# A four-layer transformer on one core: the first chunk and key weights turned on TensorE, key-phase weights kept resident, two chunks interleaved in the query phase, background matmuls on column tiles

## Chip, core, metric

The kernel runs on one core of one Trainium2 chip. The metric is device time in microseconds (us), the median of the runs; lower is better. The kernel before takes 2942.88 us (2942.56 to 2943.19, two runs).

PE is TensorE, ACT ScalarE, DVE VectorE. A "PSUM bank" is, in this kernel, one of the eight buffers of 512 columns that matmuls write to.

## The reference, cut to what matters

Four layers, A B A B, over x of 2048 rows by 1024 columns in bf16, 32 heads of 32. Both kinds have residuals and a layer norm.

```python
def _A_ref(x, wqkv, w_phi, wo):            # linear attention
    q, k, v = split(x @ wqkv)
    pq = einsum("bhsd,hdf->bhsf", q, w_phi); pk = the same of k
    phi_q = concat([softmax(pq), softmax(-pq)]); phi_k = the same of pk
    kv = einsum("bhsf,bhsd->bhfd", phi_k, v);  z = phi_k summed over s
    o = (phi_q @ kv) / (phi_q . z + 1e-6)
    return o @ wo

def _B_ref(x, wqkv, wo):                   # ordinary attention
    p = softmax(q @ k.T * Dh**-0.5)
    return (p @ v) @ wo

x = x + A(layernorm(x)); x = x + B(layernorm(x)); x = x + A(...); x = x + B(...)
```

I call an A with the B behind it one layer pair; there are two. The rows are handled in four chunks of 512.

## The kernel before

Each pair has a *key phase* (A's keys and values of all chunks), a *query phase* (A's queries, then B's projections), and *attention* (B). The first key phase runs alone at the start; the second pair's is done in the background of the first pair's attention. Attention consists of 512 steps per pair. One step is eight score matmuls S, two exponentials of 128x1024 on ACT, and sixteen matmuls ND that give numerators and denominators. Between S and ND of each step, PE takes some *background* work from a list of generators:

```python
LAYOUT = {"wide": (0, 8), "mid": (2, 3), "narrow": (3, 1)}   # score buffers of two banks, background banks

def ps512(dt=F32):                        # the next background bank
    PS["ring"] += 1
    return ps_tile(f"BG{PS['ring'] % PS['nb']}", ...)[:]

def mm8(ps, lhsT, rhs):                   # a block: 8 matmuls of 128x128 by 512 columns
    for po in range(G):
        PE.matmul(ps, lhsT=lhsT(po), rhs=rhs(po), start=(po == 0), stop=(po == G - 1))
        if po == 3:
            yield 4, False                # half done; (units of work, has a tile ended?)

def pump(self, per):                      # once per step
    self.credit = min(self.credit + per, 8.0)
    ends = 0
    while self.credit > 0 and ends < max(1, PS["nb"] - 1):
        got = self.next()
        if got is None:
            return
        self.credit -= got[0]
        ends += got[1]
...
for _ in block:                           # attend(): a step has just issued its S
    bg.pump(per)
    if len(att.lag) > 1:
        att.finish()                      # the ND of an earlier step
```

A unit of work is about one matmul of 512 columns; a tile *ends* when its bank is full and another engine can empty it. The attention layout "narrow" has three score buffers (six banks), one bank for ND and one for background. S uses tiles of 32 rows of the array (`tile_position=(32*j, 0)`), ND tiles of 32 columns (`(0, 32*j)`), background the whole array. Where a later stage needs background that isn't done, `bg.until(name)` runs the rest with no scores beside it. I call that stretch *bare*.

The start loads the first chunk and the key weights transposed, by DMA, alternating between two issuing queues, and the key phase loads its weight slabs (1 MB each) again for every chunk:

```python
def load_first(c):
    x = T("x", [P, G, C], BF16)
    for po in range(G):
        (SC if c == 0 and po % 2 else SP).dma_start_transpose(out=x[:, po, :], in_=A_x[0, ...])
    return x
...
xs = {0: load_first(0)}; load_phi(); wkT = fold_load(D, SC)    # fold_load: 8 more transposes, on SC
for c in range(NCH):
    sl = Slabs(["av", "pk"][:1 if c == 0 else 2])             # loads value and key slabs
```

The query phase of a chunk ends its sums with a chain of eleven small DVE instructions, among them one reciprocal of 3.35 us; nothing else is ready for PE in the meantime:

```python
DVE.tensor_copy(out=sdc[:], in_=sd)                        # aq_gen
...
DVE.reciprocal(out=t1[q0, :], in_=t1[q0, :])
...
DVE.tensor_tensor(out=ab[q3, :], in0=t2[q2, :], in1=ab[q2, :], op=ALU.subtract)
yield 8, True
yield from wait(6)
```

The softmax here doesn't subtract the row's maximum and nothing guards it: scores larger than these inputs give would overflow.

## Time and profile before

The head of the page gives the span and each engine's busy time, share of the span and number of instructions. No engine is busy throughout.

```profile
span 2935.6 us, 69119 instructions
...
PE 2365.3 (81%) x29739; PEld 1044.6 (36%) x30080; DVE 1336.3 (46%) x2205; ACT 2141.0 (73%) x2465; POOL 96.1 (3%) x87
```

A share over the whole span says little here, because the stages have different limits. I cut the trace at the score exponentials, which stand in a fixed order, and asked for each engine's busy time in each stage. First pair of the kernel before; columns: stretch, its length, busy us and instruction count of each engine, granted clock, DMA share, GB/s.

```profile
0.00:71.80 71.80, 8.25 (x17) 1.94 (x18) 9.55 (x67) 5.55 (x9) 0.86 (x9) 1.00 0.46 103
71.80:238.70 166.90, 150.28 (x931) 80.03 (x946) 115.20 (x185) 86.81 (x144) 47.52 (x38) 0.95 0.71 216
238.70:322.80 84.10, 69.40 (x290) 28.67 (x295) 50.01 (x80) 19.86 (x35) 0.00 (x0) 0.87 0.38 128
322.80:417.70 94.90, 77.82 (x928) 32.89 (x941) 44.24 (x77) 69.97 (x80) 0.00 (x0) 0.89 0.34 104
417.70:493.10 75.40, 67.34 (x301) 28.84 (x307) 38.52 (x61) 1.34 (x3) 0.00 (x0) 0.93 0.55 178
493.10:703.10 210.00, 173.73 (x2569) 74.61 (x2607) 81.42 (x148) 187.23 (x210) 0.00 (x0) 0.95 0.35 111
703.10:856.30 153.20, 122.25 (x1722) 52.41 (x1749) 73.36 (x139) 129.07 (x146) 0.00 (x0) 0.90 0.37 116
856.30:889.00 32.70, 23.34 (x126) 9.69 (x120) 8.97 (x13) 0.04 (x1) 0.00 (x0) 1.00 0.51 153
```

The reader should see four kinds of stretch. The start (first line) has nothing busy. The key and query phases (second and third) are PE's. The fifth and eighth lines are bare: ACT does next to nothing. In between, ACT and PE share. ACT alone would need about 1.85 us per step; 160 steps (lines six to eight) took 396 us, not 296.

What holds the start is told by the chain that ended last, in order of time (start, us, what):

```profile
11.40 2.56 DMA x<-in_A_x_dram
...
13.97 2.58 DMA x<-in_A_x_dram
...
27.03 3.27 DMA kv<-in_A_wqkv_dram
...
31.49 2.79 DMA x<-in_A_x_dram
```

One transpose lands, and only then does the next, from the other queue, begin: 2.6 us each. The Trainium skill, "DMA: Bandwidth & Descriptors", section "Silent corruption: two transposing streams in flight at once", says that the later of two transposing streams must wait for the earlier one's full completion. The trace agrees: the transpose of 11.40 us ends at 13.96, and the next begins at 13.97.

Last, one step of the first block (layout "mid"), PE alone (start, us, line, out<-in, count):

```profile
354.59 0.40 PE L534 MATMUL S<-q,kv 32*128 32x256 bf16 x8
354.92 1.90 PE L163 MATMUL BG<-c,w 128*128 128x512 bf16 x8
356.75 0.29 PE L561 MATMUL ND<-E,kv 128*32 128x256 bf16 x4
...
357.31 0.40 PE L534 MATMUL S<-q,kv 32*128 32x256 bf16 x8
```

The step takes 2.71 us. Between the start of the last background matmul and the first ND, the trace has 0.309 us (the median of the 673 such places after 400 us), though a matmul of 512 columns takes 0.216.

### The profile page before, as it was taken

How to read it: one execution, taken by the hardware profiler on the slowest of the kernel's cores; microseconds unless marked ns; L12 is line 12 of the kernel's file. 1: busy time of each engine (PE TensorE's matmuls, PEld its weight loads, DVE VectorE, ACT ScalarE, POOL GpSimd, SP SyncE). 2: the span in 40 equal slices, each digit the busy share in tenths (PEclk: the TensorE clock that was granted, in tenths of full speed). 3: DMA queues.
4: the chain of work that ended last, by engine and by line, in shares of the span. 5: the costliest groups of instructions: out<-in, count | busy, mean ns of one | idle time of the engine just before them, and what ended most of it. 6: DMA issues, size and time to landing. Idle time of an engine off the chain costs nothing.

```text
span 2935.6 us, 69119 instructions
## 1 busy us (share of the span) xinstructions
PE 2365.3 (81%) x29739; PEld 1044.6 (36%) x30080; DVE 1336.3 (46%) x2205; ACT 2141.0 (73%) x2465; POOL 96.1 (3%) x87
## 2 busy tenths in 40 slices
PE   1897978789777888888878797878978778988877
PEld 0453333333333333333333333333333333333333
DVE  1676454433546744454522745444254573322212
ACT  0552542889858888898996346188986699999996
POOL 0230000000000001010100100000000000000000
PEclk9998989999898998998999898999989899999999
DMA  4862616234253432323212261633424432321110
GB/s 101 241 213 85 194 62 197 76 129 138 67 165 111 122 127 87 120 79 114 73 45 101 79 194 59 197 93 123 134 75 147 125 97 100 105 73 59 45 45 16
DMA packets 259090, 323.98 MB, mean 110 GB/s; under 512 B 49568, under 2 KB 223648, under 8 KB 251616
## 3 DMA queue, kind: packets, MB, share of 16 engines
q1 hardware_dynamic: 248160, 316.93, 33.8%
q8 instruction: 235, 3.85, 0.5%
q10 hardware_dynamic: 10624, 2.62, 0.5%
q14 instruction: 71, 0.58, 0.1%
HBM read 252.77 MB, written 58.33 MB: 106 GB/s over the span
## 4 chain that ended last, share of the span: by engine, by line
PE 51%; ACT 18%; DVE 16%; DMA 6%; issue 5%; SPq 3%; ACTq 1%; DVEq 0%; POOLq 0%; POOL 0%
PE BG L163 28%; ACT E L543 16%; PE ND L561 10%; PE S L534 9%; DVE rc L599 3%; DMA dn<-den_d 2%; SPq L501 2%; DVE c L180 2%; DMA x<-in_A_x_dram 1%; PE BG L197 1%; DVE st L191 1%; PE BG L310 1%; ACT ea L376 1%; DVE f L397 1%; DMA den_d<-dt 1%
## 5 line engine op out<-in xcount | busy, mean ns | idle before, releaser
L543 ACT ACTIVATE E<-S 128x1024 bf16<-128x1024 f32 x2048 | 1909.3, 1116 | 408.2 <-PE S L534 407.3
L561 PE MATMUL ND<-E,kv 128*32 128x256 bf16 x8192 | 652.8, 288 | 249.5 <-DVE dt L581 77.1
L163 PE MATMUL BG<-c,w 128*128 128x512 bf16 x2371 | 591.3, 385 | 59.2 <-issue 20.2
L534 PE MATMUL S<-q,kv 32*128 32x256 bf16 x8192 | 564.2, 284 | 78.6 <-ACT E L543 40.7
L561 PE MATMUL ND<-E,ones 128*32 128x256 bf16 x8192 | 586.5, 286 | 0.0
L561 PEld LDWEIGHTS <-kv 128*32 128x32 bf16 x8192 | 266.5, 97 | 655.6 <-issue 523.5
L163 PE MATMUL BG<-w,c 128*128 128x512 bf16 x1442 | 355.6, 387 | 34.9 <-DVE st L463 12.4
L163 PEld LDWEIGHTS <-w 128*128 128x128 bf16 x2560 | 228.4, 99 | 342.9 <-issue 126.6
L534 PEld LDWEIGHTS <-kv 32*128 32x128 bf16 x8192 | 169.8, 92 | 408.5 <-issue 406.0
L561 PEld LDWEIGHTS <-ones 128*32 128x32 bf16 x8192 | 262.3, 99 | 5.1
L599 DVE RECIPROCAL rc<-nd 128x256 f32<-128x256 f32 x128 | 224.4, 1753 | 4.4
L163 PEld LDWEIGHTS <-c 128*128 128x128 bf16 x1536 | 142.4, 99 | 212.1 <-issue 60.7
L440 DVE TENSOR_TENSOR x<-BG,x 128x512 bf16<-128x512 f32 x128 | 88.4, 691 | 191.2 <-PE BG L163 190.8
L592 DVE COPY nd<-ND 128x512 f32<-128x512 f32 x64 | 44.1, 689 | 261.8 <-PE ND L561 261.3
L294 POOL TENSOR_TENSOR ea<-ea,sm 128x512 bf16<-128x512 bf16 x64 | 93.8, 1465 | 791.8 <-ACT E L543 339.6
L189 ACT ACTIVATE st<-c 128x512 bf16<-128x512 bf16 x56 | 31.5, 622 | 118.2 <-DMA xa_d<-c 65.0
L412 DVE TENSOR_TENSOR ea<-BG,ea 128x512 bf16<-128x512 f32 x128 | 84.7, 686 | 56.5 <-PE BG L411 38.7
L376 ACT ACTIVATE ea<-f 128x512 bf16<-128x512 f32 x128 | 75.3, 660 | 39.9 <-DVE f L373 39.8
L197 PE MATMUL BG<-st,ones 128*128 128x512 bf16 x121 | 48.5, 489 | 67.1 <-ACT st L189 51.0
L288 DVE TENSOR_REDUCE sm<-ea 128x32 f32<-128x1024 bf16 x64 | 77.8, 1216 | 53.1 <-ACT ea L284 35.3
L373 DVE TENSOR_TENSOR f<-BG,r 128x512 f32<-128x512 f32 x64 | 44.0, 691 | 125.8 <-PE BG L163 125.8
L463 DVE TENSOR_SCALAR st<-BG,rcol 128x512 bf16<-128x512 f32 x64 | 48.0, 751 | 97.5 <-PE BG L163 97.5
(79 smaller groups left out, 1238.4 us busy)
## 6 DMA issues: line engine op xcount, KB each, us to landing
w<-in_B_wqkv_dram SPq DMA_DIRECT2D x48, 1024.0 KB
dn<-den_d SPq DMA_DIRECT2D x320, 64.0 KB
w<-in_A_wqkv_dram SPq DMA_DIRECT2D x16, 1024.0 KB
x_d<-x SPq DMA_DIRECT2D x16, 1024.0 KB
x<-x_d SPq DMA_DIRECT2D x16, 1024.0 KB
w<-wpq_d SPq DMA_DIRECT2D x16, 1024.0 KB
w<-in_A_wo_dram SPq DMA_DIRECT2D x16, 1024.0 KB
w<-in_B_wo_dram SPq DMA_DIRECT2D x16, 1024.0 KB
```

Source lines behind the costliest of these rows:

```text
L163: PE.matmul(ps, lhsT=lhsT(po), rhs=rhs(po), start=(po == 0), stop=(po == G - 1))
L180: DVE.tensor_tensor(out=xc[:, po, :], in0=x[:, po, :], in1=m[:], op=ALU.subtract)
L197: PE.matmul(ps, lhsT=ones_bf[:], rhs=sqs[po], start=(po == 0), stop=(po == G - 1))
L288: DVE.reduce_sum(out=ss[:], in_=e[:].rearrange("p s (h f) -> p s h f", f=DH), axis=AX.X)
L294: (POOL if s else DVE).tensor_tensor(out=e[:, s, :].rearrange("p (h f) -> p h f", f=DH), in0=e[:, s, :].rearrange("p (h f) -> p h f", f=DH ...
L376: SC.activation(out=e[:, s, :], in_=pq[:], func=ACT.Exp, scale=1.0 - 2.0 * s)
L412: DVE.tensor_tensor(out=es[g][:, s, :], in0=ps, in1=es[g][:, s, :], op=ALU.mult)
L440: DVE.tensor_tensor(out=x[:, ft, :], in0=ps, in1=x[:, ft, :], op=ALU.add)
L534: PE.matmul(tiles[j // 2][:, o:o + QH], lhsT=kv[rows, 0, (kc + k) * P:(kc + k + 1) * P], rhs=q[rows, g, half * QH:(half + 1) * QH], start= ...
L543: SC.activation(out=e[:], in_=tiles[i][:].rearrange("p (j k q) -> p j k q", k=2, q=QH), func=ACT.Exp, scale=SCALE,)
L561: PE.matmul(nd[rows, part * QH:(part + 1) * QH], lhsT=ones_bf[:, 0:32] if part else kv[:, 1, col:col + 32], rhs=es[j // 2][:, j % 2, i, :] ...
L599: DVE.reciprocal(out=rc[:], in_=ndc[:, QH:C])
```

## The change

Its intent, in five parts: (1) the first chunk is loaded in rows and turned on TensorE, the key weights too; (2) the key phase's slabs stay in memory; (3) the query phase is cut into parts, so that chunk 1's exponents fill chunk 0's waits, and less is left to the background of the first block; (4) background beside attention runs as four tiles of 32 columns, the shape of ND; (5) the background is paced differently: three tile ends per step in "mid", and in the first 96 of the 160 narrow steps 5 units per step instead of 4, with chunks 2 and 3 queued together. A few smaller edits come with it (some query-phase results are emptied by ACT and no longer by DVE, the query weights are loaded one chunk earlier).

```diff
+    def mm(ps, lhsT, rhs, start, stop):
+        if PS["ns"] == 0:
+            PE.matmul(ps, lhsT=lhsT, rhs=rhs, start=start, stop=stop, skip_group_check=True)
+            return
+        for j in range(4):
+            cols = slice(32 * j, 32 * j + 32)
+            PE.matmul(ps[cols, :], lhsT=lhsT[:, cols], rhs=rhs, start=start, stop=stop,
+                      tile_position=(0, 32 * j), skip_group_check=True)
 ...
-            while self.credit > 0 and ends < max(1, PS["nb"] - 1):
+            while self.credit > 0 and ends < PS["nb"]:
 ...
-        xs = {0: load_first(0)}
-        wkT = fold_load(D, SC)
+        wn = [T("q", [P, 4, D], BF16) for _ in range(2)]    # key weights, as they lie
+        av = [T("kv", [P, G, C], BF16) for _ in range(2)]   # resident value and
+        pk = [T("w", [P, G, C], BF16) for _ in range(2)]    # folded key slabs
+        ...  # plain loads; load_first(0) and fold_k turn them with PE.transpose
-            main = ak_gen(c, xs[c], sl, True, res, hook)
+            main = ak_gen(c, xs[c], iter(av + pk).__next__, True, res, hook)
 ...
-            drain(to_b(0, (0,), True))
 ...
+            drain(aq_exp(xr0, wpq, es0))
+            exp1 = aq_exp(xr1, wpq, es1)
+            drain(aq_scale(es0, r0))
+            for _ in range(8):
+                next(exp1)
 ...
+            drain(merge(aq_out(es0, r0), exp1, 6))
+            drain(aq_scale(es1, r1))
+            drain(aq_finish(0, x0, r0["sl"], r0))
 ...
             bg.add("b2", to_b(2))
+            bg.add("b3", to_b(3))
-            attend(att, att.block(qs[0], 4, 8, acc[0], None, False, False), bg, 4)
-            attend(att, att.block(qs[1], 0, 8, acc[1], None, True, False), bg, 4)
+            attend(att, att.block(qs[0], 4, 8, acc[0], None, False, False), bg, 5)
+            attend(att, att.block(qs[1], 0, 8, acc[1], None, True, False), bg, 5)
             bg.until("b2")
-            bg.add("b3", to_b(3))
```

More of the change, by code (lines that the diff above doesn't have):

```diff
@@ L153, in ps512 @@
         PS["ring"] += 1
-        return ps_tile(f"BG{PS['ring'] % PS['nb']}", C if dt == F32 else P, dt)[:]
+        return ps_tile(f"BG{PS['ring'] % PS['nb']}", C, dt)[:]
     def wait(n):
@@ L159, in wait @@
             yield 0, True
+    def mm(ps, lhsT, rhs, start, stop):
[4 more added lines that the diff above has]
+            cols = slice(32 * j, 32 * j + 32)
+            PE.matmul(
+                ps[cols, :], lhsT=lhsT[:, cols], rhs=rhs, start=start, stop=stop,
+                tile_position=(0, 32 * j), skip_group_check=True,
+            )
     def mm8(ps, lhsT, rhs):
         for po in range(G):
-            PE.matmul(ps, lhsT=lhsT(po), rhs=rhs(po), start=(po == 0), stop=(po == G - 1))
+            mm(ps, lhsT(po), rhs(po), po == 0, po == G - 1)
             if po == 3:
@@ L196, in ln_gen @@
         for po in range(G):
-            PE.matmul(ps, lhsT=ones_bf[:], rhs=sqs[po], start=(po == 0), stop=(po == G - 1))
+            mm(ps, ones_bf[:], sqs[po], po == 0, po == G - 1)
             if po < G - 1 and po % 2:
@@ L234, in flush_kv, with ak_gen @@
             yield from pending.pop(0)()
-    def ak_gen(c, x, slabs, fast=False, res=None, hook=None):
+    def ak_gen(c, x, get, fast=False, res=None, hook=None):
         if c == 0:
@@ L239, in ak_gen @@
         kvacc = kv_state["acc"]
-        slabs.prefetch()
         if res is None:
@@ L252, in ak_gen @@
         for fc in range(2):
-            w = slabs.get()
+            w = get()
             for t in range(4):
@@ L267, in ak_gen @@
         for fc in range(2):
-            w = slabs.get()
+            w = get()
             es = []
@@ L309, in kv_part @@
                         for s in range(2):
-                            PE.matmul(
+                            mm(
                                 ps[:, s * 129:(s + 1) * 129],
-                                lhsT=es[t][:, s, gi * P:(gi + 1) * P],
-                                rhs=va[t // 2][:, t % 2, g, :],
-                                start=(t == 0 and s == 0), stop=(t == 3),
-                                skip_group_check=True,
+                                es[t][:, s, gi * P:(gi + 1) * P],
+                                va[t // 2][:, t % 2, g, :],
+                                t == 0 and s == 0, t == 3,
                             )
@@ L354, in kv_finish, with aq_load @@
         yield 0, True
-    def aq_gen(c, x, slabs, res, fast=False):
-        kvs, zs = kv_state["m"], kv_state["z"]
+    def aq_load(c):
         xc = T("c8", [P, G, C], BF16)
@@ L362, in aq_gen, with aq_exp @@
         SP.dma_start(out=rstd[:], in_=ra_d[c][:])
-        slabs.prefetch()
-        es = []
+        return xc, rstd
+    def aq_exp(xr, ws, es):
+        xc, rstd = xr
         for g in range(G):
-            if g % 4 == 0:
-                w = slabs.get()
+            if callable(ws):
+                w = ws() if g % 4 == 0 else w
+            else:
+                w = ws[g // 4]
             ps = ps512()
@@ L373, in aq_gen, with aq_scale @@
             DVE.tensor_tensor(out=pq[:], in0=ps, in1=rstd[:], op=ALU.mult)
-            e = T("ea", [P, 2, C], BF16)
             for s in range(2):
-                SC.activation(out=e[:, s, :], in_=pq[:], func=ACT.Exp, scale=1.0 - 2.0 * s)
-            es.append(e)
+                SC.activation(out=es[g][:, s, :], in_=pq[:], func=ACT.Exp, scale=1.0 - 2.0 * s)
             yield 4, True
+    def aq_scale(es, res):
+        zs = kv_state["z"]
         sd = ps512()
@@ L381, in aq_gen @@
             for s in range(2):
-                PE.matmul(
-                    sd[64 * s:64 * (s + 1), :], lhsT=zs[:, s, g, :], rhs=es[g][:, s, :],
-                    start=(g == 0), stop=(g == G - 1), tile_position=(0, 64 * s),
-                    skip_group_check=True,
-                )
+                for k in range(2):
+                    o = 64 * s + 32 * k
+                    PE.matmul(
+                        sd[o:o + 32, :], lhsT=zs[:, s, g, 32 * k:32 * k + 32],
+                        rhs=es[g][:, s, :], start=(g == 0), stop=(g == G - 1),
+                        tile_position=(0, o), skip_group_check=True,
+                    )
+            if g == 3:
+                yield 4, False
         sdc = T("f", [P, C], F32)
@@ L391, in aq_gen @@
         ab = T("ab", [P, C], BF16)
+        res["ab"] = ab
         q0, q1, q2, q3 = (slice(32 * i, 32 * i + 32) for i in range(4))
-        DVE.tensor_copy(out=sdc[:], in_=sd)
+        (SC.copy if PS["ns"] == 0 else DVE.tensor_copy)(out=sdc[:], in_=sd)
         DVE.tensor_tensor(out=t1[q0, :], in0=sd[q1, :], in1=sdc[q2, :], op=ALU.mult)
@@ L403, in aq_gen, with aq_out @@
         DVE.tensor_tensor(out=ab[q3, :], in0=t2[q2, :], in1=ab[q2, :], op=ALU.subtract)
-        yield 8, True
-        yield from wait(6)
-        oT = T("c8", [P, G, C], BF16)
+        yield 4, True
+    def aq_out(es, res):
+        kvs, ab = kv_state["m"], res["ab"]
+        oT = res["oT"] = T("c8", [P, G, C], BF16)
+        act = PS["ns"] == 0
         def bcast(g):
@@ L410, in bcast @@
                 ps = ps512()
-                PE.matmul(ps, lhsT=Rsel[:, g, s, :], rhs=ab[:], start=True, stop=True)
+                mm(ps, Rsel[:, g, s, :], ab[:], True, True)
                 DVE.tensor_tensor(
@@ L422, in aq_gen, with aq_finish @@
             for s in range(2):
-                PE.matmul(
-                    ps, lhsT=kvs[s][:, g, :], rhs=es[g][:, s, :], start=(s == 0), stop=(s == 1)
-                )
-            (SC.copy if fast else DVE.tensor_copy)(out=oT[:, g, :], in_=ps)
+                mm(ps, kvs[s][:, g, :], es[g][:, s, :], s == 0, s == 1)
+            (SC.copy if act else DVE.tensor_copy)(out=oT[:, g, :], in_=ps)
             yield 2, True
-        yield from proj_out(x, oT, slabs)
-        yield from ln_gen(x, res, fast)
+    def aq_gen(c, x, slabs, res, pause=6):
+        xr = aq_load(c)
+        slabs.prefetch()
+        es = [T("ea", [P, 2, C], BF16) for _ in range(G)]
+        yield from aq_exp(xr, slabs.get, es)
+        yield from aq_scale(es, res)
+        yield from wait(pause)
+        yield from aq_out(es, res)
+        yield from aq_finish(c, x, slabs, res)
+    def aq_finish(c, x, slabs, res):
+        yield from proj_out(x, res["oT"], slabs)
+        yield from ln_gen(x, res, PS["ns"] == 0)
         SP.dma_start(out=x_d[c][:], in_=x[:])
@@ L462, in bkv_gen @@
             )
-            DVE.tensor_scalar(
-                out=st[:, :, t, :], in0=ps.rearrange("p (g d) -> p g d", d=P),
-                scalar1=rcol[:, t:t + 1], scalar2=None, op0=ALU.mult,
+            scale_rows(
+                st[:, :, t, :], ps.rearrange("p (g d) -> p g d", d=P), rcol[:, t:t + 1],
+                PS["ns"] == 0,
             )
@@ L571, in finish @@
             if not last:
-                a = acc[0][g][:, acc[1], half, :]
+                a = acc[0][g // 2][:, g % 2, half, :]
                 if half == 0:
@@ L594, in finish @@
                 DVE.tensor_tensor(
-                    out=ndc[:, 0:QH], in0=num, in1=acc[0][g][:, acc[1], half, :], op=ALU.add
+                    out=ndc[:, 0:QH], in0=num, in1=acc[0][g // 2][:, g % 2, half, :], op=ALU.add
                 )
@@ L679, in run, with loads @@
         set_mode("wide")
-        xs = {0: load_first(0)}
+        wn = [T("q", [P, 4, D], BF16) for _ in range(2)]
+        av = [T("kv", [P, G, C], BF16) for _ in range(2)]
+        pk = [T("w", [P, G, C], BF16) for _ in range(2)]
+        xs = {}
+        res = {}
+        def loads():
+            SP.dma_start(out=av[0][:], in_=W["av"](0))
+            for k in range(2):
+                (SC if k else SP).dma_start(
+                    out=wn[k][:], in_=A_w[:, 4 * k:4 * k + 4, D:2 * D]
+                )
+            SP.dma_start(out=av[1][:], in_=W["av"](1))
+        xs[0] = load_first(0)
         load_phi()
-        wkT = fold_load(D, SC)
-        res = {}
+        loads()
         drain(ln_gen(xs[0], res, True))
@@ L686, in run @@
             nres = {}
-            sl = Slabs(["av", "pk"][:1 if c == 0 else 2])
             hook = None
             if c == 0:
-                hook = lambda sl=sl: fold_phi(wkT, wpk_d, sl)
-            if c == 2:
-                wqT = fold_load(0, SP)
+                hook = lambda: fold_k(wn, pk)
+            if c == 1:
+                wqT = [T("q", [P, 4, D], BF16) for _ in range(2)]
+                for g in range(G):
+                    SP.dma_start_transpose(
+                        out=wqT[g // 4][:, g % 4, :], in_=A_wqkv[:, g * P:(g + 1) * P]
+                    )
             if c == 3:
-                hook = lambda: fold_phi(wqT, wpq_d, None)
-            main = ak_gen(c, xs[c], sl, True, res, hook)
+                hook = lambda: fold_q(wqT)
+            main = ak_gen(c, xs[c], iter(av + pk).__next__, True, res, hook)
             if c + 1 < NCH:
@@ L709, in after @@
             if layer == 0:
-                yield from ak_gen(c, x, sl, fast)
+                yield from ak_gen(c, x, sl.get, fast)
                 SP.dma_start(out=x_d[c][:], in_=x[:])
@@ L723, in run @@
             drain(kv_finish())
-            tiles = [T(f"acc{g}", [P, 2, 2, QH], F32) for g in range(G)]
-            acc = [(tiles, 0), (tiles, 1)]
             qs = {}
@@ L730, in run, with to_b, b_proj @@
             BKVQ = ["bk0", "bv0", "bq0", "bk1", "bv1", "bq1"]
-            def to_b(c, parts=(0, 1), fast=False):
-                if 0 in parts:
-                    x = load_x(c)
-                    res = saved[c] = {}
-                    sl = res["sl"] = Slabs(["pq", "ao"] + (BKVQ if c < 2 else BKV))
-                    yield from aq_gen(c, x, sl, res, fast)
-                    if c < 2:
-                        qs[c] = T("q", [P, G, C], BF16)
+            def to_b(c):
+                x = load_x(c)
+                res = saved[c] = {}
+                sl = res["sl"] = Slabs(["pq", "ao"] + BKV)
+                yield from aq_gen(c, x, sl, res)
+                yield from b_proj(c, (0, 1))
+                SP.dma_start(out=xb_d[c][:], in_=res["xc"][:])
+                SP.dma_start(out=rb_d[c][:], in_=res["rstd"][:])
+            def b_proj(c, parts):
                 res = saved[c]
@@ L742, in to_b, with rest1 @@
                     yield from bkv_gen(c, res, res["sl"], h, qs.get(c))
-                if c >= 2:
-                    SP.dma_start(out=xb_d[c][:], in_=res["xc"][:])
-                    SP.dma_start(out=rb_d[c][:], in_=res["rstd"][:])
-            drain(to_b(0, (0,), True))
+            x0 = load_x(0)
+            r0, r1 = {}, {}
+            saved[0], saved[1] = r0, r1
+            r0["sl"] = Slabs(["ao"] + BKVQ)
+            r1["sl"] = Slabs(["ao"] + BKVQ)
+            sp = Slabs(["pq"])
+            xr0 = aq_load(0)
+            sp.prefetch()
+            wpq = sp.ready
+            es0 = [T("ea", [P, 2, C], BF16) for _ in range(G)]
+            early = [T(f"acc{4 + k}", [P, 2, 2, C], BF16) for k in range(4)]
+            es1 = [early[g // 2][:, g % 2] for g in range(G)]
+            xr1 = aq_load(1)
+            drain(aq_exp(xr0, wpq, es0))
[3 more added lines that the diff above has]
+                next(exp1)
+            r0["sl"].prefetch(1)
+            drain(merge(aq_out(es0, r0), exp1, 6))
+            drain(aq_scale(es1, r1))
+            drain(aq_finish(0, x0, r0["sl"], r0))
+            qs[0] = T("q", [P, G, C], BF16)
+            qs[1] = T("q", [P, G, C], BF16)
+            drain(b_proj(0, (0,)))
+            def rest1():
+                yield from aq_out(es1, r1)
+                x1 = load_x(1)
+                yield from aq_finish(1, x1, r1["sl"], r1)
+                yield from b_proj(1, (0, 1))
             bg = Background()
             set_mode("mid")
-            bg.add("b0", to_b(0, (1,)))
-            bg.add("b1", to_b(1))
+            bg.add("b0", b_proj(0, (1,)))
+            bg.add("b1", rest1())
+            acc = [([T(f"acc{k}", [P, 2, 2, QH], F32) for k in range(4)], 0), None]
             attend(
@@ L758, in run @@
             bg.until("b1")
+            acc[1] = ([T(f"acc{4 + k}", [P, 2, 2, QH], F32) for k in range(4)], 1)
             set_mode("narrow")
             bg.add("b2", to_b(2))
-            attend(att, att.block(qs[0], 4, 8, acc[0], None, False, False), bg, 4)
-            attend(att, att.block(qs[1], 0, 8, acc[1], None, True, False), bg, 4)
+            bg.add("b3", to_b(3))
+            attend(att, att.block(qs[0], 4, 8, acc[0], None, False, False), bg, 5)
+            attend(att, att.block(qs[1], 0, 8, acc[1], None, True, False), bg, 5)
             bg.until("b2")
-            bg.add("b3", to_b(3))
             attend(att, att.block(qs[0], 8, 12, acc[0], None, False, False), bg, 6)
@@ L812, with pe_transpose @@
     phi = T("t16", [P, G, P], BF16)
-    def fold_load(base, eng):
-        wT = [T("kv", [P, 4, D], BF16) for _ in range(2)]
-        for g in range(G):
-            eng.dma_start_transpose(
-                out=wT[g // 4][:, g % 4, :], in_=A_wqkv[:, base + g * P:base + (g + 1) * P]
-            )
-        return wT
-    def fold_phi(wT, dst, slabs):
-        ws = [T("w", [P, G, C], BF16) for _ in range(2)]
-        for hh in range(2):
-            for m in range(G):
-                ps = ps512()
-                for gi in range(4):
-                    PE.matmul(
-                        ps[:, gi * P:(gi + 1) * P],
-                        lhsT=wT[hh][:, gi, m * P:(m + 1) * P], rhs=phi[:, hh * 4 + gi, :],
-                        start=True, stop=True, skip_group_check=True,
-                    )
-                (DVE.tensor_copy if m % 2 else SC.copy)(out=ws[hh][:, m, :], in_=ps)
-                yield 1, True
-            SP.dma_start(out=dst[:, :, hh * C:(hh + 1) * C], in_=ws[hh][:])
-        if slabs is not None:
-            slabs.ready += ws
+    def pe_transpose(dst, src, k):
+        ps = ps512(BF16)
+        for i in range(4):
+            PE.transpose(out=ps[:, i * P:(i + 1) * P], in_=src(i), identity=ident[:])
+        (SC.copy if k % 2 else DVE.tensor_copy)(out=dst, in_=ps)
@@ new lines, in fold_k @@
+    def fold_k(wn, ws):
+        for hh in range(2):
+            wT = T("c8", [P, 4, D], BF16)
+            for gi in range(4):
+                o = (hh * 4 + gi) * P
+                for k in range(2):
+                    pe_transpose(
+                        wT[:, gi, k * C:(k + 1) * C],
+                        lambda i: wn[k][:, i, o:o + P], gi * 2 + k,
+                    )
+                    yield 1, True
+            yield from fold_mm(wT, hh, lambda m: ws[hh][:, m, :])
+            SP.dma_start(out=wpk_d[:, :, hh * C:(hh + 1) * C], in_=ws[hh][:])
@@ new lines, in fold_mm, with fold_q @@
+    def fold_mm(wT, hh, dst):
+        for m in range(G):
+            ps = ps512()
+            for gi in range(4):
+                PE.matmul(
+                    ps[:, gi * P:(gi + 1) * P],
+                    lhsT=wT[:, gi, m * P:(m + 1) * P], rhs=phi[:, hh * 4 + gi, :],
+                    start=True, stop=True, skip_group_check=True,
+                )
+            (DVE.tensor_copy if m % 2 else SC.copy)(out=dst(m), in_=ps)
+            yield 1, True
+    def fold_q(wT):
+        for hh in range(2):
+            st = T("st", [P, 4, C], BF16)
+            st2 = T("st", [P, 4, C], BF16)
+            yield from fold_mm(wT[hh], hh, lambda m: (st, st2)[m // 4][:, m % 4, :])
+            for i, t in enumerate((st, st2)):
+                SP.dma_start(out=wpq_d[:, 4 * i:4 * i + 4, hh * C:(hh + 1) * C], in_=t[:])
@@ L849, in load_first @@
         x = T("x", [P, G, C], BF16)
+        if c:
+            for po in range(G):
+                SP.dma_start_transpose(
+                    out=x[:, po, :], in_=A_x[0, c * C:(c + 1) * C, po * P:(po + 1) * P]
+                )
+            return x
+        rows = [T("ea", [P, D], BF16) for _ in range(4)]
+        for t in range(4):
+            (SC if t % 2 else SP).dma_start(out=rows[t][:], in_=A_x[0, t * P:(t + 1) * P, :])
         for po in range(G):
-            (SC if c == 0 and po % 2 else SP).dma_start_transpose(
-                out=x[:, po, :], in_=A_x[0, c * C:(c + 1) * C, po * P:(po + 1) * P]
-            )
+            pe_transpose(x[:, po, :], lambda i: rows[i][:, po * P:(po + 1) * P], po)
         return x
@@ L864, in store_out @@
             for po in range(G):
-                ps = ps512(BF16)
+                ps = ps512(BF16)[:, 0:P]
                 PE.transpose(out=ps, in_=x[:, po, t * P:(t + 1) * P], identity=ident[:])
```

## The prediction

Its "layer" is a layer pair, and its "value products" are ND.

> **What bounds it now.** The page shows ACT busy 73%, PE 81%. I cut the trace at the score exponentials (2048 of 128x1024, one every 0.93 us back to back: 1.86 us per attention step of two).
>
> | stage | us, layer 1 / 2 | bound by |
> |---|---|---|
> | start to first projection | 72 / - | serial DMA transposes, 2.6 us each |
> | key phase | 167 / - | PE; two 7 us waits for reloaded key weights |
> | query phase to first score | 84 / 89 | PE, a DVE chain of 10 us |
> | first block (32 steps) | 170 / 170 | PE; last 75 us have no scores |
> | next 160 steps | 396 / 399 | ACT and PE; last 33 us have no scores |
> | last 320 steps | 688 / 612 | ACT, 1.86-2.2 us per step |
>
> **Start and key phase.** The chain of waits shows 63 us of DMA transposes alternating between two queues. After: plain row loads (about 10 us beside weights), 32 PE transposes with 8 evictions of 0.6-0.7 us on two engines, the first norm: projections start near 27 us. Transposes on one queue alone issued at 1.4 us each, so chunk 1 arrives about when needed. Costs: 16 more evictions (+5 us), fold staging (+3). Gain: the two reload waits, 14 us. Net -48.
>
> **Query phase and first block.** 80 matmuls of 0.216 us (chunk 1's exponents and sums) leave the background and fill the DVE chain: wide stage +8 per layer. The first block's background then starts at chunk 1's output (three tile ends per step, not two); its projection fits under the 32 steps, so about 24 blocks of 8 matmuls, 41 us, plus some norm stay bare instead of 75 us. The 8 us score stall behind the reciprocal goes. -40. Net -32 per layer.
>
> **Column tiles.** A group of four 128x32 matmuls of 256 columns takes 0.112 us in a run; after a change of tile shape the next group starts 0.205 us later, so a change costs 95 ns. Trainium skill, "TensorEngine Tiling (Array Packing)", Key Properties, says a mode change drains the engine; this trace agrees. A step with background has three changes, then two: 95 ns in about 690 steps, worth something only where PE sets the step. The page's Restrictions say column tiling disables fast weight load; existing column-tiled work hides its loads, so I expect four 512-column tiles in 0.216 us, no loss.
>
> **160 steps.** Both chunks queued together, 5 units instead of 4: chunk 2's bare 5 us goes, chunk 3 starts earlier, bare end 33 to 15 us. With fewer changes, -26 per layer. Last 320 steps: -12 and -3.
>
> **Sum.** -48 -64 -52 -15 = -179; a little off for unforeseen collisions: **2775 us**, range 2700 to 2840. Faster 0.94, same 0.05, slower 0.01.
>
> **What shows it right.** First projection near 27 us; no wait for key weights; first score near 280 us; first blocks near 130 us; four column tiles in 0.216 us and 0.21 us from background to value products (0.309 now); bare end halved.
>
> **What would make it wrong.** Chunk 1's transposes stuck behind 3-4 MB of loads; four-way 512-column tiles slower than 0.216 us; 5 units lengthening steps more than the bare end saves (scores have three buffers); DVE backlog holding the one background bank.

## The result

The changed kernel takes 2831.71 us (2830.72 to 2832.70, two runs), 111 us less; the ratio is 0.9622, 95% interval 0.9581 to 0.9664. Ratios in this document are the mean time of one kernel's runs over the mean of the other's in the same rounds, so they are not quite the ratio of the medians quoted. The forecast was 2775 us, range 2700 to 2840. All outputs are right.

The head of the changed kernel's page:

```profile
span 2830.9 us, 89391 instructions
...
PE 2375.8 (84%) x40048; PEld 1151.2 (41%) x40048; DVE 1326.5 (47%) x2205; ACT 2156.5 (76%) x2489; POOL 95.7 (3%) x87
```

The stretches that answer to those of before, in the same order:

```profile
0.00:22.70 22.70, 10.69 (x48) 5.21 (x49) 11.38 (x71) 8.47 (x13) 0.85 (x9) 0.90 0.94 263
22.70:188.00 165.30, 152.97 (x1009) 82.67 (x1008) 117.57 (x190) 90.70 (x152) 47.16 (x38) 0.96 0.55 159
188.00:282.60 94.60, 84.77 (x414) 35.47 (x416) 60.03 (x95) 31.73 (x56) 0.00 (x0) 0.94 0.32 103
282.60:369.60 87.00, 79.84 (x1580) 38.02 (x1576) 49.00 (x93) 63.35 (x66) 0.00 (x0) 0.94 0.47 150
369.60:412.50 42.90, 42.10 (x796) 20.06 (x792) 17.83 (x26) 0.04 (x1) 0.00 (x0) 1.00 0.62 189
412.50:624.80 212.30, 185.77 (x3724) 93.09 (x3720) 84.44 (x153) 192.68 (x221) 0.00 (x0) 0.96 0.38 123
624.80:786.60 161.80, 122.45 (x2380) 58.26 (x2376) 73.34 (x138) 124.56 (x137) 0.00 (x0) 0.88 0.34 108
786.60:805.10 18.50, 13.57 (x240) 6.58 (x236) 4.73 (x7) 0.03 (x2) 0.00 (x0) 1.00 0.47 148
```

The start shrank by 49 us, the first block's bare stretch (fifth line) from 75 to 43, the bare stretch of the last line from 33 to 18.5. But lines six and seven, the steps with scores, got longer. All stages of both profiled runs, in us, with the change that the prediction gave:

| stage | before, pair 1 / 2 | after, pair 1 / 2 | change | predicted |
|---|---|---|---|---|
| start and key phase | 238.7 | 188.0 | -50.7 | -48 |
| up to the first score (pair 2: from pair 1's last) | 84.1 / 152.4 | 94.6 / 162.7 | +10.5 / +10.3 | +8 / +8 |
| first block, 32 steps | 170.3 / 170.2 | 129.8 / 130.1 | -40.5 / -40.1 | -40 / -40 |
| next 160 steps | 395.9 / 398.8 | 392.6 / 398.9 | -3.3 / +0.1 | -26 / -26 |
| last 320 steps | 687.9 / 612.2 | 690.4 / 616.2 | +2.5 / +4.0 | -12 / -3 |
| after the last score | 25.3 | 27.5 | +2.2 | 0 |

The first three rows came as forecast, within a few us. The lower ones are the whole shortfall: they were to give 67 us and gave nothing.

The changed step of the first block:

```profile
300.25 0.40 PE L567 MATMUL S<-q,kv 32*128 32x256 bf16 x8
300.58 1.91 PE L169 MATMUL BG<-w,c 128*32 128x512 bf16 x32
302.31 0.28 PE L594 MATMUL ND<-E,kv 128*32 128x256 bf16 x4
...
302.86 0.40 PE L567 MATMUL S<-q,kv 32*128 32x256 bf16 x8
```

Thirty-two tiles take as long as eight whole matmuls did, so four tiles run side by side. ND starts 1.73 us after the background now, not 1.83, and the step takes 2.61 us instead of 2.71. Over all steps after 400 us the median from the last background matmul's start to ND fell from 0.309 to 0.204 us. So the mechanism of the tiles is as forecast. A step of the narrow layout with eight background matmuls, though, took 2.71 us before (PE; one of the eight is missing in the trace):

```profile
808.77 0.40 PE L534 MATMUL S<-q,kv 32*128 32x256 bf16 x8
809.10 1.90 PE L163 MATMUL BG<-c,w 128*128 128x512 bf16 x7
...
811.48 0.40 PE L534 MATMUL S<-q,kv 32*128 32x256 bf16 x8
```

and still takes 2.71 us after the change (PE and, in the first line, DVE; in brackets the idle time before):

```profile
529.20 0.69 DVE L473 TENSOR_TENSOR x<-BG,x 128x512 bf16<-128x512 f32 x1 [2.90 <-PE BG L169]
...
529.51 0.40 PE L567 MATMUL S<-q,kv 32*128 32x256 bf16 x8
529.94 1.91 PE L169 MATMUL BG<-c,w 128*32 128x512 bf16 x32
...
532.22 0.40 PE L567 MATMUL S<-q,kv 32*128 32x256 bf16 x8
```

DVE empties the one background bank from 529.20 to 529.89, and the next block starts at 529.94: 0.43 us after S, not 0.33 as in the first block. The 0.1 us that the tiles saved is waited out there.

For comparison, a narrow step with four background matmuls in the kernel before, 1.84 us:

```profile
599.43 0.40 PE L534 MATMUL S<-q,kv 32*128 32x256 bf16 x8
599.76 1.04 PE L163 MATMUL BG<-c,w 128*128 128x512 bf16 x4
...
601.27 0.40 PE L534 MATMUL S<-q,kv 32*128 32x256 bf16 x8
```

To see what a step costs by what it carries, I cut both traces at the first score matmul of each step and counted the background matmuls up to the next (four tiles as one; in the trace of before a few records are missing, so seven counts as eight and three as four). Pair 1, medians:

| steps | before | after |
|---|---|---|
| chunk 1's 64 steps among the 160, 4 matmuls | 1.85 us | 1.84 us |
| the same, 8 matmuls | 3 steps only | 2.71 us |
| last 32 of the 160, 8 matmuls | 2.71 us | 2.71 us |
| steps with 8 matmuls among the 160 | 20 | 34 |

Four matmuls fit beside a step that ACT sets; four more cost 0.86 us, 0.215 us each, the full price. Of chunk 1's 34 steps with four matmuls, 14 took PE only 1.74 or 1.75 us after the change: there the tiles' 0.1 us shows, but the two exponentials of a step still take ACT 1.82 us (median). The change took 18.2 us out of the bare stretches of pair 1 (37.5 to 19.3 us) and made 14 more steps carry eight matmuls: 14 x 0.86 = 12.0 us, beside 14.9 us that the steps with scores in fact got longer. It moved the work; it did not hide it. (The table leaves out the 32 narrow steps of chunk 0 that come first; ten of them carry four matmuls after the change and took 2.38 us, for which I give no cause.)

### The profile page after: what moved, and what is told of

Same layout as the page of the kernel before. It is cut to its first block, busy times and chain, and to the rows that moved or that the text cites. A ratio compares the mean times of both kernels' runs of the same rounds, so it can differ in the third digit from the quotient of the medians.

```text
span 2830.9 us, 89391 instructions
## 1 busy us (share of the span) xinstructions
PE 2375.8 (84%) x40048; PEld 1151.2 (41%) x40048; DVE 1326.5 (47%) x2205; ACT 2156.5 (76%) x2489; POOL 95.7 (3%) x87
## 5 line engine op out<-in xcount | busy, mean ns | idle before, releaser
L169 PE MATMUL BG<-c,w 128*32 128x512 bf16 x7680 | 482.1, 385 | 33.4 <-DVE x L473 14.7
L594 PEld LDWEIGHTS <-kv 128*32 128x32 bf16 x8192 | 278.7, 99 | 496.0 <-issue 311.5
L169 PEld LDWEIGHTS <-w 128*32 128x32 bf16 x7680 | 191.4, 97 | 240.1 <-issue 107.2
L169 PE MATMUL BG<-w,c 128*32 128x512 bf16 x3328 | 212.9, 388 | 12.1 <-DVE st L239 5.1
L165 PE MATMUL BG<-c,w 128*128 128x512 bf16 x640 | 150.6, 396 | 1.6 <-DVE nd L625 1.6
L169 PEld LDWEIGHTS <-c 128*32 128x32 bf16 x3328 | 83.8, 97 | 105.3 <-issue 46.8
L165 PEld LDWEIGHTS <-c 128*128 128x128 bf16 x704 | 69.3, 99 | 86.3 <-issue 6.6
L165 PE MATMUL BG<-w,c 128*128 128x512 bf16 x448 | 99.4, 383 | 2.0 <-ACT st L924 2.0
L165 PEld LDWEIGHTS <-w 128*128 128x128 bf16 x640 | 64.5, 101 | 85.3 <-issue 17.5
L486 DVE TENSOR_TENSOR st<-BG,r 128x512 bf16<-128x512 f32 x64 | 44.2, 691 | 97.7 <-PE BG L169 93.3
```

The costliest lines, as they stand in the source:

```text
L165: PE.matmul(ps, lhsT=lhsT, rhs=rhs, start=start, stop=stop, skip_group_check=True)
L169: PE.matmul(ps[cols, :], lhsT=lhsT[:, cols], rhs=rhs, start=start, stop=stop, tile_position=(0, 32 * j), skip_group_check=True,)
L486: DVE.tensor_tensor(out=st[:, gi, :], in0=ps, in1=rstd[:], op=ALU.mult)
L594: PE.matmul(nd[rows, part * QH:(part + 1) * QH], lhsT=ones_bf[:, 0:32] if part else kv[:, 1, col:col + 32], rhs=es[j // 2][:, j % 2, i, :] ...
```

## The experiments

Twelve runs in four jobs; the runs of a job share a chip and its runs of the kernel before. query_in_background, one_queue, bare_banks, chain_parts ran on another chip than the yardstick below, so are compared with the yardstick only through their ratios to the kernel before.

### The changed kernel again: after_again

No edit.

> The changed kernel unaltered, as the yardstick for the other runs of this job. Every theory: 2831 us again, within 0.2%.

2825.37 us (2824.60 to 2833.13), ratio 0.9617 (0.9604 to 0.9631). This is the yardstick for the other runs. One hundredth of the ratio is 29 us; the intervals are 4 to 6 us either way.

### Whole array for all background: full_array

```diff
-        if PS["ns"] == 0:
+        if True:
             PE.matmul(ps, lhsT=lhsT, rhs=rhs, start=start, stop=stop, skip_group_check=True)
```

> The changed kernel with every background matmul on the full array again. Theory A (a change of tile shape costs PE 95 ns, but that shows in the time only in the first block's 8-matmul steps: 22 per layer; 4-matmul steps are set by ACT at 1.85 us; 8-matmul steps of the narrow layout by the round trip of the one background bank, 7 x 0.216 + 1.19 = 2.70 us, tiled or not): +4 to +8 us, 2835 to 2840; 8-matmul steps of the first block 2.71 instead of 2.61 us, of the later 160 steps 2.71 as now. Rival B (the 690 saved changes are all worth their 95 ns and something else ate the gain): +40 to +66 us, 2870 to 2900. Rival C (the tiles do harm, by four times the instructions and the 129-column products): below 2825.

2838.59 us, ratio 0.9654 (0.9641 to 0.9668): about 11 us slower than the yardstick. Rivals B and C are out. The first block's steps with eight matmuls went back to 2.71 us, the narrow ones stayed at 2.71. Theory A stands, its size a little too small: the first blocks account for 4.8 us (132.7 and 131.9 us against 129.0 and 130.8). The profiled execution was the fastest of this kernel (2832.07 us), only 6 us above the yardstick's profiled one, so its trace leaves about 1 us of its own difference open. Where the rest of the 11 us lies in the slower executions no trace shows.

### Four units per step: four_units

```diff
-            attend(att, att.block(qs[0], 4, 8, acc[0], None, False, False), bg, 5)
-            attend(att, att.block(qs[1], 0, 8, acc[1], None, True, False), bg, 5)
+            attend(att, att.block(qs[0], 4, 8, acc[0], None, False, False), bg, 4)
+            attend(att, att.block(qs[1], 0, 8, acc[1], None, True, False), bg, 4)
```

> The changed kernel with 4 instead of 5 units of background per step in the first 96 of the 160 steps. Theory A (zero sum: a matmul above four in a step costs 0.86 / 4 = 0.215 us there, and in the bare end, with one bank, 2.70 / 8 = 0.34 us): fewer 8-matmul steps, a bare end longer by about as much or more, total +2 to +16 us, 2833 to 2847. Rival B (5 units lengthen the steps for nothing and are why the 160 steps gained nothing): -16 to -24 us, 2807 to 2815.

2823.91 us, ratio 0.9610 (0.9594 to 0.9627): no different from the yardstick. In pair 1, the steps with eight matmuls fell from 34 to 19, and the bare stretches grew from 19 to 38 us (7.9 and 30.5). The 160 steps took 394.0 and 390.6 us in the two pairs, against 392.4 and 397.7. Rival B's 16 to 24 us are out: five units did no such harm. They did no good either. Theory A is right that the sum is about zero (-2 us, uncertain by 6), but its size, +2 to +16 us, was missed: that bare work is dearer does not show in the total.

### Two tile ends per step: two_ends

```diff
-            while self.credit > 0 and ends < PS["nb"]:
+            while self.credit > 0 and ends < max(1, PS["nb"] - 1):
```

> The changed kernel with two tile ends per step in the first block, not three. Theory A (the output stage then takes 12 steps instead of 8, four steps' worth of projection, 32 matmuls, moves to the bare end): first blocks longer by 4 to 7 us, total +8 to +14 us, 2839 to 2845. Rival B (DVE sets these steps; the third end only lengthens them): within 2 us of the changed kernel.

2842.86 us, ratio 0.9673 (0.9659 to 0.9686): about 16 us slower, a little more than theory A's range. The first blocks took 138.0 and 138.2 us instead of 129.0 and 130.8. The third end per step is worth having.

### Chunk 1's exponents back in the background: query_in_background

```diff
-            exp1 = aq_exp(xr1, wpq, es1)
             drain(aq_scale(es0, r0))
-            for _ in range(8):
-                next(exp1)
 ...
-            drain(merge(aq_out(es0, r0), exp1, 6))
-            drain(aq_scale(es1, r1))
+            drain(aq_out(es0, r0))
 ...
             def rest1():
 ...
+                yield from aq_exp(xr1, r1["sl"].get, es1)
+                yield from aq_scale(es1, r1)
+                yield from wait(6)
                 yield from aq_out(es1, r1)
```

> The changed kernel with chunk 1's query exponents and sums back in the first block's background; column tiles and three ends stay. Theory A (filling the DVE chain of chunk 0 is what made the first block short): stage before the first score shorter by 8 to 10 us per layer, first block longer by 26 to 32 us; total +36 to +48 us on the changed kernel's 2827, so 2863 to 2875. Rival B (the first block is short for its third tile end and its column tiles): within 16 us, below 2843.

2874.25 us, ratio 0.9775 (0.9753 to 0.9796): 46 us slower than the yardstick's ratio. The first score came at 270.9 us instead of 282.3, and the first blocks took 163.5 and 163.2 us. Theory A holds: interleaving the two chunks costs 11 us before the first score and saves some 33 us behind it, for each pair. It is the largest part of the gain beside the start.

### The kernel before, all transposes on one queue: one_queue

```diff
-            (SC if c == 0 and po % 2 else SP).dma_start_transpose(
+            SP.dma_start_transpose(
 ...
-        wkT = fold_load(D, SC)
 ...
                 xs[c + 1] = load_first(c + 1)
+                if c == 0:
+                    wkT = fold_load(D, SP)
```

> The kernel BEFORE with one edit: all its DMA transposes of the start are issued on one queue, in the order chunk 0, chunk 1, key weights, instead of alternating on two. Nothing is turned on TensorE. Theory A (the 63 us of the start were the alternation: 1.4 us per transpose on one queue, not 2.6): first projection at 25 to 35 us instead of 72, total -30 to -42 us on the kernel before, 2898 to 2910, so most of the changed start's gain without TensorE. Rival B (a DMA transpose costs its 2.6 us whatever the queue, and only TensorE avoids it): first projection after 50 us, total -20 us at most.

2908.82 us, ratio to before 0.9883 (0.9867 to 0.9900), 34 us faster than before without TensorE turning anything. Issues on the SP queue (start, us, count):

```profile
0.74 12.96 SPq L852 DMA_TRANSPOSE x<-in_A_x_dram  x10
...
16.11 7.64 SPq L852 DMA_TRANSPOSE x<-in_A_x_dram  x6
23.80 10.82 SPq L818 DMA_TRANSPOSE kv<-in_A_wqkv_dram  x8
```

Twenty-four transposes are issued within 34 us, one every 1.3 us while they run. Theory A's reason is right, but the first projection still came only at 41.5 us, not at 25 to 35: PE waited 19.0 us for a weight slab (engine, waited for, us, times, longest), issued behind all of these.

```profile
PE BG L163 <- DMA w<-in_A_wqkv_dram: 19.0, 1, 19.0
```

### And the first value slabs issued at once: one_queue_slabs

```diff
+        sl0 = Slabs(["av"], SC)          # issued on the other queue
+        sl0.prefetch()
 ...
-            sl = Slabs(["av", "pk"][:1 if c == 0 else 2])
+            sl = Slabs(["av", "pk"]) if c else sl0
```

> The kernel BEFORE with its DMA transposes on one queue, as in one_queue, and its first two value weights issued at once on the other queue, so that they don't wait behind 24 transposes (they were issued at 35 us and PE waited 19 us for them). Theory A (one queue of transposes is enough; what remained was the order of loads): first projection at 23 to 28 us, as with TensorE, total -45 to -54 us on the kernel before, 2887 to 2896. Rival B (plain loads beside transposes slow both, or chunk 1 and the key weights now come late): first projection after 33 us or as much lost later, 2900 to 2910.

2903.45 us, ratio 0.9871 (0.9852 to 0.9890). The first projection came at 23.9 us, as early as with TensorE (22.7), and the key projection of chunk 0 at 51.5 us, earlier than with TensorE (56.1). But the total is not clearly better than one_queue's. Rival B's second half was right: 7.0 us for a reloaded value slab and 11.0 us for reloaded key slabs were waited for later:

```profile
PE BG L164 <- DMA w<-wpk_d: 11.0, 2, 6.3
...
PE BG L164 <- DMA w<-in_A_wqkv_dram: 7.0, 1, 7.0
```

That is what the resident slabs of the change are for, so an early start and resident slabs go together. What resident slabs alone are worth, without the early start, no run shows.

### Idle score buffers for bare background: bare_banks

```diff
     def ps512(dt=F32):
         PS["ring"] += 1
+        if PS.get("bare") and dt == F32 and PS["ring"] % 4:
+            PS["sring"] += 1
+            return ps_tile(f"S{PS['sring'] % PS['ns']}", 2 * C)[:, 0:C]
 ...                                       # until():
+            PS["bare"] = PS["mode"] == "narrow"
```

> The changed kernel, but where the narrow layout runs background with no scores at all, its products also use the three idle score buffers, not the one bank alone. Theory A (a block of 8 costs 2.70 us there for the round trip of the one bank, 1.73 us if PE never waits): the bare end of 18.5 us falls to 12 or 13, total -10 to -16 us, 2811 to 2817. Rival B (weights arriving or DVE bound the bare end): within 3 us of 2827.

2818.18 us, ratio 0.9580 (0.9565 to 0.9594): 11 us below the yardstick's ratio. Bare blocks of the changed kernel first, then of this one (PE):

```profile
789.05 1.91 PE L169 MATMUL BG<-c,w 128*32 128x512 bf16 x32 [0.79 <-DVE st L486]
791.75 1.91 PE L169 MATMUL BG<-c,w 128*32 128x512 bf16 x32 [0.79 <-DVE st L486]
794.45 1.91 PE L169 MATMUL BG<-w,c 128*32 128x512 bf16 x32 [0.79 <-DVE st L486]
```

```profile
790.45 3.64 PE L172 MATMUL S<-c,w 128*32 128x512 bf16 x64
793.90 1.91 PE L172 MATMUL S<-w,c 128*32 128x512 bf16 x32
795.63 1.91 PE L172 MATMUL BG<-w,c 128*32 128x512 bf16 x32
```

With one bank, blocks start 2.70 us apart, because PE waits until DVE has emptied it; with the idle score buffers, 1.73 us. The bare end fell from 18.5 to 13.3 us in pair 1. Theory A holds, at the lower end of its range; rival B's 3 us are out.

### The DVE chain in four parts: chain_parts

```diff
+        part = PS["ns"] > 0
+        if part:
+            yield 1, True
         DVE.reciprocal(out=t1[q0, :], in_=t1[q0, :])
+        if part:
+            yield 1, True
 ...                                       # one more further on
-    def aq_gen(c, x, slabs, res, pause=6):
+    def aq_gen(c, x, slabs, res, pause=3):
```

> The changed kernel with the DVE chain of the query sums cut into four parts over four steps in the narrow layout (the pause after it shortened by three), so that score sums can be read between the parts. Theory A (the chain holds the one bank of value products for 8.2 us, and ACT starves 7.6 us, once for each of chunks 2 and 3 per layer): -14 to -24 us, 2803 to 2813. Rival B (the time comes back as background that ends later, zero sum): within 4 us of 2827.

2813.35 us, ratio 0.9559 (0.9539 to 0.9579): 17 us below the yardstick's ratio, theory A's size. The waits of ND in the 32 steps in which chunk 0 meets the keys of chunk 2 (pair 1), in the changed kernel and then here (us in total, times, longest):

```profile
PE ND L594 <- DVE dt L614: 20.1, 11, 10.2
```

```profile
PE ND L601 <- DVE dt L621: 14.3, 10, 3.5
```

The longest wait fell from 10.2 to 3.5 us. The stretch took 71.3 and 69.7 us in the two pairs, against 76.0 and 77.7 in after_again. All 160 steps took 386.9 and 387.8 us, against 392.4 and 397.7, with the bare end at 18.5 us as before: the time did not come back there, and rival B is out. The pause after the chain went from six steps to three, which makes up for the three steps that the parts take; the two edits were not run apart.

### Both mends: both, both_again

> The changed kernel with both mends that gained: idle score buffers for background without scores (-9 us measured), the DVE chain in four parts (-13 to -17 us measured). Theory A (they act on different stretches): the sum, 2800 to 2808 us, ratio to before 0.952 to 0.955. Rival B (the chain's gain was only background pushed to the bare end, which the other mend shortens anyway): 2810 to 2816, no better than the chain alone.

2799.17 us (2796.37 to 2802.63), ratio 0.9521 (0.9505 to 0.9538). The gains add up, as theory A has it. This is the fastest kernel, 1% below the changed one.

> The changed kernel with both mends, again, as the yardstick for the other run of this job: 2799 us, ratio to before 0.950 to 0.954.

In another job on the same chip 2799.86 us, ratio 0.9529 (0.9510 to 0.9547): the same. Nine of the ten runs of the kernel before in this ratio are those of the job of both.

### Both mends, nothing turned on TensorE: both_one_queue

```diff
-        wn = [T("q", [P, 4, D], BF16) for _ in range(2)]
+        wkT = [T("q", [P, 4, D], BF16) for _ in range(2)]
 ...                                       # value slabs on the other queue, at once
+                if c == 0:
+                    for g in range(G):
+                        SP.dma_start_transpose(out=wkT[g // 4][:, g % 4, :], in_=A_wqkv[...])
 ...                                       # fold_k and load_first(0) without PE.transpose
```

> The same with nothing turned on TensorE: chunk 0 and the key weights come by DMA transposes on one queue, key-phase slabs still kept resident, value weights issued at once on the other queue. Theory A (the start's gain was one queue, load order and resident slabs; TensorE turning itself is worth nothing): first projection at 23 to 26 us, key projection of chunk 0 at 50 to 53 us instead of 56, first score within 5 us of both_again's 283.7, total within 6 us of it. Rival B (TensorE turning is needed to be this early, because 40 us of transposes hold back the loads of chunks 2 and 3): total 10 to 30 us slower.

2804.18 us (2795.54 to 2807.69), ratio 0.9533 (0.9515 to 0.9550), against 0.9529: no difference. The first projection came at 24.2 us, the key projection of chunk 0 at 51.3, the first score at 279.4 us against 282.4 in both_again (the 283.7 of the expectation was that of both). Theory A holds: turning on TensorE is one way not to alternate queues, and no better than one queue with the loads in the right order.

## Why the prediction was right, and where it fell short

**Start and key phase: right in size (-50.7, forecast -48), and the reason is now shown.** The alternation of two queues cost the time. TensorE itself gave nothing that one queue would not give. The resident slabs matter: without them 18 us of the early start is waited for again. The split was less exact than the sum: the first projection came at 22.7 us, not 27, while the key phase itself shrank by 1.6 us (166.9 to 165.3) only. The prediction counted 14 us for two reload waits, the length of the loads in the chain; PE waited 8.1 us for them in the trace of before.

**Query phase and first block: right.** +10 and -40 per pair, forecast +8 and -40. The run that put the exponents back lost 46 us; the run with two ends lost 16.

**Column tiles: the mechanism right, the place wrong.** One change of tile shape fewer per step, 0.105 us by the medians of the trace (the prediction's 95 ns subtract a distance counted from a group's first matmul, 0.112, from one counted from its last, 0.205); four tiles in 0.216 us; no loss from the weight loads. The prediction said that this is worth something only where PE sets the step, and then counted it in stages where PE doesn't: steps with four matmuls take as long as ACT's exponentials (1.85 us), and narrow steps with eight wait for the one bank. Undoing the tiles everywhere cost 11 us, not tens.

**The 160 steps: here a step failed.** "Both chunks queued together, 5 units instead of 4: chunk 2's bare 5 us goes, chunk 3 starts earlier, bare end 33 to 15 us. With fewer changes, -26 per layer." The bare stretches shrank as said (5 to 1 us, 33 to 18.5). The failed step is that the work moved out of them was counted as free: 5 and 18 us of bare time make 23 of the 26. It went into steps that had no room: each matmul beyond four cost 0.215 us. Measured: -3.3 and +0.1 us. The prediction named this danger ("5 units lengthening steps more than the bare end saves") but did not price it, though 2.71 against 1.85 us could have been read from the trace of before.

**The last 320 steps.** "-12 and -3" measured +2.5 and +4.0. Hardly anything but the tiles changes there, and most of these steps are ACT's. I don't give a cause to the few us that they seem slower: full_array shows no clear difference in these stages, and the second profile of the changed kernel has 688.0 and 615.9 us, against 687.9 and 612.2 before. What is shown is that the 15 us did not come.

In the sum the forecast was 57 us too fast but in its range. Of the 168 us forecast, 111 came; the terms for the later steps, 67 us, came to nothing. So the result fell into the range thanks to the range's width, 8 us below its upper end, and not because every term was right. Every sign on the prediction's list came true, the halved bare end too; but a shorter bare end is a gain only if the steps that take its work do not grow.

## What to carry to other kernels

Price a moved piece of work by the stretch that it moves into, not by the one that it leaves: find the steps' capacity first (here four matmuls per step), and expect full price beyond it. A change that frees an engine shows in the time only if no other limit stands close behind; here the round trip of a single PSUM bank stood 0.1 us behind. Before moving transposes to another engine, look whether two queues are taking turns.

## What the Trainium skill lacked or had wrong

- "TensorEngine Tiling (Array Packing)", Key Properties: it says that a change of tiling mode drains the engine, without a figure. Here it cost about 0.105 us: in the trace of before, the next group starts 0.110 us after the start of a group of four ND tiles of 256 columns in a run, and 0.216 us after it where scores S, of the other shape, follow (medians).
- The same page, Restrictions: column tiling disables fast weight load. Whatever that costs elsewhere, nothing of it shows here: 32 load and matmul pairs of 32 columns by 512 took 1.73 us, as eight whole ones would.
- "TensorE: Matmul & The Clock Gate", section "Back-to-back issue gap": it gives about 131 ns per matmul of 512 columns for a sustained stream of load and matmul pairs, and calls its formula's 216 ns an over-count. In the trace of before such streams start every 216 ns. For 128 columns it gives about 81 ns; 32 pairs of 129 columns took 1.82 us here, 57 ns each. The page's own walk through a matmul has 215.7 and 55.6 ns, measured, and that is what the trace bears out.
- "DMA: Bandwidth & Descriptors", section "Silent corruption: two transposing streams in flight at once": it says that streams must wait for one another, but not what alternating costs: 2.6 us per transpose of 128x512 on two queues in turn, 1.3 us on one.
- "Perfetto Trace Analysis", Matmuls, advises to rotate through several PSUM banks, and no page says what a single bank costs. Blocks of eight matmuls start 2.70 us apart with one bank that DVE empties in 0.69 us, and 1.73 us apart with several.
